# A fused attention, expert and feed-forward kernel: narrowed pieces from two places, the third pass's first weights prepared later, squares and casts one unit later

## The chip, the cores and the metric

The kernel runs on one core of a Trainium2 chip. The metric is the device time of one execution in microseconds. Engines are named as in the profile: PE (TensorE, with PEld for its weight loads), DVE (VectorE), ACT (ScalarE), POOL (GpSimd) and SP (SyncE, whose queue issues the DMAs).

## The reference

Attention with masks, an expert layer whose experts all see every token, and a feed-forward layer with squared ReLU, on 2304 tokens of width 512:

```python
x = attention(q, k, v)                     # 4 batches, 8 heads, 576 positions, 64 wide
P = exp(x @ w_gate - max); 8 times: P /= P.sum(1); P /= P.sum(0); P *= N / 8
for e in range(8):                         # w1[e]: 512 x 1024, w2[e]: 1024 x 512
    out += P[:, e:e+1] * (np.maximum(x @ w1[e], 0) @ w2[e])
r = np.maximum(out @ w_in, 0)              # w_in: 512 x 2048, given in float64
return (r * r) @ w_out                     # w_out: 2048 x 512, given in float64
```

## The kernel before, in words

**Passes and steps.** After attention the work is 80 steps. Steps 0 to 31 are the expert layer for a first 1024 tokens and a "single" group of 256 tokens (pass 1), steps 32 to 63 the expert layer for the last 1024 tokens (pass 2), steps 64 to 71 and 72 to 79 the feed-forward layer for the same two groups (passes 3 and 4). In the code `NS1` is 32, `first` is [0, 32, 64, 72], and `i` is the step. Each step covers 256 hidden columns.

**Operands.** Every float32 operand is held as a rounded high part and the remainder, and a product is three matmuls. The high part is an ACT copy (`hi`), the remainder a DVE subtraction (`lo`). Products of 1024 tokens are formed by seven smaller products (u1 to u7 for the first layer, v1 to v7 for the second where it is "mixed" in the same way), whose operands need sums of blocks; POOL forms these (`s1`, `s2` for weights, `mix` for the hidden layer).

**Units and the order written by hand.** PE's work is a list of units, each mostly six matmuls of 512 columns. `order` is the list of one step. `after(k, f)` puts `f` into the program behind the k-th following unit, so for every engine the program order is set by these numbers. Each engine, and SP's queue, runs its instructions in that order; a waiting instruction holds back what stands behind it on its engine.

**Weights of a step.** `prep_w(i)` prepares step n = i + 1: from the raw block in `raw1` it makes `blk` (high and low) and, through `sums`, `sum` (high and low), in one of two sets `wset[n % 2]`, and stores them to DRAM. A pass for the second token group (`kept`) prepares nothing and fetches the four tiles that the pass before stored. Step 64's weights are an exception before the change: they are prepared at the end of pass 1 (in step 31, in the places that belong to step 32), stored, and the weights of step 32 are fetched into the same tiles behind unit 10 of step 31. At step 63 they are fetched like any others.

**Blocks of the tokens.** The seven token operands `x_hi`, `x_lo` of the next pass are fetched by `fetch_block` in the last step of a pass, 14 transfers of 512 KB. They were prepared before by `split_on`: a load, then for each block an ACT cast and behind the next unit a DVE subtraction and two stores.

**Narrowing.** The feed-forward weights come as 64-bit floats. `load_raw` loads a piece (512 columns), `narrow` makes float32 of it with seven DVE instructions in three stages, and stage 3 ends with the store (L334) to `w32`. 22 pieces (`DEEP`) are done in steps 3 to 19, one stage behind each of the units 1, 3, 5 and 7, so 3 steps hold 4 pieces and a stage 1 stands behind unit 7 in every third step. In these the result `topf` lies in the first half of the tile `deep[2]` and a second array `x` in its other half. The pieces alternate between two source tiles, `deep[0]` and `deep[1]`. Stage 1 (L310, L314) writes `topf`; stage 2 is L319 and L322, stage 3 L327, L330 and L333. The ten later pieces write `x` into the source itself, at every second word.

**Squares.** In steps 64 to 71 and 79, `evac_g` takes a hidden tile from PSUM: `positive` (ACT, L669), then `square` (two ACT instructions, L674), then `low` (DVE, L659), each one unit after the other. The tiles `r` and `g` come from a ring of three.

**Copies that PE waits for.** u1's result is copied by ACT (L755), u4's (L767) and u5's (L771) free the bank that the next of these products writes; v1's copies are L945. L871, L875 and L955 on DVE, L867 and L869 add or copy a finished bank into `acc`, which frees the bank. In step 32 two transposes of the single group (`turn`, L905, copy L918) use the bank of w0 and w1.

Of the kernel before, what the change touches and what calls it, by code (L numbers as in the profile page):

```python
# [10 lines left out]
F32 = mybir.dt.float32  # L11
F32R = mybir.dt.float32r
I32 = mybir.dt.int32
# [23 lines left out]
NS1 = E * SPE  # L37
# [13 lines left out]
def tile_kernel(ctx: ExitStack, tc: tile.TileContext, a):  # L51
# [113 lines left out]
    def prep_w(i, layers=(1, 2)):  # L165

        out = []
        tt = nc.gpsimd.tensor_tensor
        c = lambda z, k: z[:, k, :]
        flat = lambda z: z.rearrange("p b c -> p (b c)")  # L170

        def hi(w, src):
            return lambda: nc.scalar.copy(w[0], src)

        def lo(w, src, then=lambda: None):
            def f():
                nc.vector.tensor_tensor(out=w[1], in0=src, in1=w[0].bitcast(F32), op=ALU.subtract)  # L177
                then()

            return f  # L180

        n = i + 1
        late = 4 if i == 2 * NS1 else 0
        if NS1 < n <= 2 * NS1 or first[3] <= n < len(steps):
            w = wset[n % 2]
            out += [(0, lambda: fetch("blk", n, w["blk"])), (0, lambda: fetch("sum", n, w["sum"]))]
        elif 1 in layers and n < len(steps):
            w = wset[n % 2]

            def s1():  # L190
                tt(out=c(sums, 0), in0=c(raw1, 2), in1=c(raw1, 3), op=ALU.add)
                tt(out=c(sums, 2), in0=c(raw1, 0), in1=c(raw1, 2), op=ALU.subtract)

            def s2():
                tt(out=c(sums, 1), in0=c(sums, 0), in1=c(raw1, 0), op=ALU.subtract)
                tt(out=c(sums, 3), in0=c(raw1, 1), in1=c(sums, 1), op=ALU.subtract)

            def keep(name):
                if n < 2:
                    kept_back.append(lambda: store(name, n, w[name]))  # L200
                else:
                    store(name, NS1 if n == NS1 else place(n), w[name])

            def blk_done():
                if n not in (0, NS1):
                    load_w(2 * NS1 if n + 1 == NS1 else n + 1, 0)
                keep("blk")

            at = (4, 5, 6, 8) if n == NS1 else (2, 5, 10, 12) if TURN + 1 < n < NS1 else (2, 5, 10, 14) if n < NS1 else (2, 5, 8, 11)
            spread = n > first[2] + 1  # L210
            if spread:
                at = (6, 7, 14, 16)
            out += [(3 if spread else 0, s1), (4 if spread else 1, s2), (late + at[0], hi(w["blk"], flat(raw1)))]
            out += [(late + at[1], lo(w["blk"], flat(raw1), blk_done))]
            out += [(late + at[2], hi(w["sum"], flat(sums)))]
            out += [(late + at[3], lo(w["sum"], flat(sums), lambda: keep("sum")))]
            if n == NS1:
                out += [(10, lambda: fetch("blk", n, w["blk"])), (10, lambda: fetch("sum", n, w["sum"]))]
        if 2 not in layers:
            return out  # L220
        if kept(i):
            w2 = wset[i % 2]["w2"]
            out += [(0, lambda: fetch("w2", i, w2))]
            if mixed(i):
                out += [(6 if i == NS1 else 0, lambda: fetch("mix", i, mixes[i % 2]))]
            if i == 2 * NS1 - 3:
                out += [(2, lambda: load_w(2 * NS1 + 1, 0)), (2, lambda: load_w(2 * NS1, 1))]
        elif i >= 0:
            w2 = wset[i % 2]["w2"]
            moe = i < SCALED  # L230
            r = raw2.rearrange("p (f e d) -> p f e d", f=FC, e=2)
            z = mix32.rearrange("p (k d) -> p k d", k=4)

            def m1():
                tt(out=c(z, 0), in0=r[:, 0, 1], in1=r[:, 1, 1], op=ALU.add)
                tt(out=c(z, 2), in0=r[:, 0, 0], in1=r[:, 0, 1], op=ALU.subtract)

            def m2():
                tt(out=c(z, 1), in0=c(z, 0), in1=r[:, 0, 0], op=ALU.subtract)
                tt(out=c(z, 3), in0=r[:, 1, 0], in1=c(z, 1), op=ALU.subtract)  # L240
                load_w(i + 1, 1)

            def m3():
                tt(out=r[:, 1, 1], in0=r[:, 0, 1], in1=r[:, 1, 1], op=ALU.add)  # L244
                tt(out=r[:, 0, 1], in0=r[:, 0, 0], in1=r[:, 0, 1], op=ALU.subtract)

            def m4():
                tt(out=r[:, 0, 0], in0=r[:, 1, 1], in1=r[:, 0, 0], op=ALU.subtract)
                tt(out=r[:, 1, 0], in0=r[:, 1, 0], in1=r[:, 0, 0], op=ALU.subtract)

            if SCALED <= i < NS1:
                at = (7, 8, 9, 9, 14, 16) if i > TURN else (7, 8, 9, 9, 13, 15)
            elif moe:
                at = (0, 0, 0, 1, 9, 11) if i == 0 else (8, 10, 11, 12, 16, 17) if i == 1 else (1, 3, 6, 7, 13, 15)
            else:
                at = (11, 13, 14, 14, 20, 22) if late else (14, 15, 16, 16, 21, 22) if n == first[2] + 2 else (12, 13, 14, 14, 19, 20)
            if i:
                out += [(at[0], hi(w2, raw2)), (at[1], lo(w2, raw2, lambda: store("w2", place(i), w2)))]
            if moe:
                out += [(at[2], m1), (at[3], m2)]  # L260
                out += [(at[4], hi(mixes[1], mix32)), (at[5], lo(mixes[1], mix32, lambda: store("mix", place(i), mixes[1])))]
            elif i + 1 < first[3]:
                m = mixes[1]

                def mix_done():
                    load_w(i + 1, 1)
                    store("mix", place(i), m)

                out += [(at[2], m3), (at[3], m4), (at[4], hi(m, raw2)), (at[5], lo(m, raw2, mix_done))]
        else:  # L270
            w2 = wset[0]["w2"]
            out += [(6, hi(w2, raw2)), (7, lo(w2, raw2, lambda: kept_back.append(lambda: store("w2", 0, w2))))]
        return out
# [22 lines left out]
    def narrow(n):  # L296

        which, s, k = raw_pieces[n]
        src = loaded.pop(n)
        low, high = src[:, :, 0], src[:, :, 1]  # L300
        if n < DEEP:
            if len(deep) == 2:
                deep.append(xb())
            topf, x = deep[2][:, :NP], deep[2][:, NP:]
        else:
            topf, x = apart[1] if apart else xb()[:, :NP], high.bitcast(F32)
        top, bits = topf.bitcast(I32), x.bitcast(I32)

        def stage_1():
            nc.vector.tensor_scalar(  # L310
                out=top, in0=high, scalar1=3, scalar2=0x3FFFFFFF,
                op0=ALU.logical_shift_left, op1=ALU.bitwise_and,
            )
            nc.vector.scalar_tensor_tensor(  # L314
                out=top, in0=high, scalar=-0x40000000, in1=top, op0=ALU.bitwise_and, op1=ALU.bitwise_or
            )

        def stage_2():
            nc.vector.tensor_scalar(  # L319
                out=bits, in0=high, scalar1=0x7FFFFFFF, scalar2=None, op0=ALU.bitwise_and  # L320
            )
            nc.vector.scalar_tensor_tensor(  # L322
                out=topf, in0=bits, scalar=float(0x38100000), in1=topf, op0=ALU.is_ge, op1=ALU.mult
            )

        def stage_3():
            nc.vector.tensor_scalar(  # L327
                out=bits, in0=top, scalar1=-0x800000, scalar2=None, op0=ALU.bitwise_and
            )
            nc.vector.scalar_tensor_tensor(  # L330
                out=x, in0=low.bitcast(U32), scalar=2.0**-52, in1=x, op0=ALU.mult, op1=ALU.mult
            )
            nc.vector.tensor_tensor(out=topf, in0=topf, in1=x, op=ALU.add)  # L333
            nc.sync.dma_start(w32[which, s, :, NP * k:NP * k + NP], topf)  # L334
            done[0] += 1

        return [stage_1, stage_2, stage_3]
# [310 lines left out]
    def evac_g(i, ghi, glo, src, k):  # L648
# [25 lines left out]
                nc.scalar.activation(out=z, in_=held["r"], func=AF.Square)  # L674

        after(k, positive)
        after(k + 1, square)
        after(k + 2, lambda: low(held["g"], False))

    def l1_pair(i):  # L680

# [298 lines left out]
    with tc.manual_schedule():  # L980
# [218 lines left out]
        for i in range(len(steps) + 1):  # L1199
# [23 lines left out]
            if mixed(i - 1):  # L1223
# [4 lines left out]
                    names = "v1 u1 v2 us v6 v5 u2 u3 v7 u4 v3 u5 v4 u6 u7"  # L1228
                elif i == NS1:
                    u |= zip(("w0", "w1"), l2s)  # L1230
                    names = "v1 u1 v2 w0 v6 w1 v5 u2 u3 v7 u4 v3 u5 v4 u6 u7"
                elif i in (first[1] - 1, first[2] - 1, len(steps) - 1):
                    names = "u1 v1 u2 v2 u3 u4 v6 u5 v5 u6 u7 v7 v3 v4"
                else:
# [39 lines left out]
            elif NS1 + 4 <= i < 2 * NS1 - 4:  # L1274
                split_on(1, 5, 9)
            elif 2 * NS1 < i < 2 * NS1 + 7:
                for k in {2 * NS1 + 1: (3, 8, 16), 2 * NS1 + 6: (2, 5, 8, 12, 16)}.get(i, (3, 16)):
                    split_on(2, k, k + 1)
            if i == first[2] - 2:
                for k, f in enumerate(operands_single()):  # L1280
# [109 lines left out]
```

## Time and profile before

| | us |
|---|---|
| median of 3 runs | 1959.26 |
| lowest, highest | 1959.09, 1964.13 |
| the profiled execution, its own time | 1961.56 |
| its span, first to last instruction | 1959.8 |
| granted clock over the span, share of full | 0.991 |

Times within a trace are counted from the start of the span. "Busy" is the time in which an engine executes; a gap in brackets is idle time of the engine before an instruction, with what ended it. PE's matmuls overlap, so that a matmul of 512 columns is shown as about 0.39 us although the next starts some 0.23 us after it. Windows were cut where the first matmul of a step starts.

### The profile page before, as it was taken

To read this page: it belongs to the slowest core of one execution; us is meant where nothing else is said; L and a number is where in the kernel's file an instruction comes from. 1 tells how busy PE (TensorE), PEld (TensorE's weight loads), DVE (VectorE), ACT (ScalarE), POOL (GpSimd) and SP (SyncE) were. 2 spreads that over 40 slices of the span, in tenths; PEclk is the share of its full clock that TensorE was granted. 3 is DMA by queue.
4 is the path that set the end of the run, shared out by engine and by line. 5 is a ranking of instruction groups with operands and counts; after the bars stand their busy time and mean duration, and the time that the engine had idled before them with its cause. 6 is when DMAs were issued, how large, how long until landed. Compare 5 with 4: busy or idle time off the path is not lost.

```text
span 1959.8 us, 28254 instructions
## 1 busy us (share of the span) xinstructions
PE 1902.1 (97%) x10343; PEld 1566.9 (80%) x10343; DVE 1614.9 (82%) x2424; ACT 816.0 (42%) x1354; POOL 672.6 (34%) x584
## 2 busy tenths in 40 slices
PE   8998999899999999999899999999999999999999
PEld 6777878778777888888688888888888887878887
DVE  6786877778686699999678998998999998785896
ACT  6753333233233344444243433333333365553444
POOL 3532322322332355555232433423233344330331
PEclk9999999999999999999999999999999999999999
DMA  8685767676676466666976667667576787879671
GB/s 296 224 312 190 254 223 249 234 264 234 228 254 220 166 219 222 218 223 225 389 290 241 258 252 266 242 262 280 196 260 247 299 319 285 293 280 395 230 251 67
DMA packets 162554, 492.75 MB, mean 251 GB/s; under 512 B 16928, under 2 KB 32176, under 8 KB 162416
## 3 DMA queue, kind: packets, MB, share of 16 engines
q1 hardware_dynamic: 162416, 490.96, 69.1%
q8 instruction: 81, 1.33, 0.3%
q14 instruction: 57, 0.47, 0.1%
HBM read 282.15 MB, written 208.74 MB: 250 GB/s over the span
## 4 chain that ended last, share of the span: by engine, by line
PE 62%; DVE 4%; DMA 1%; issue 1%; POOL 1%; ACT 1%; POOLq 0%; SPq 0%; DVEq 0%; ACTq 0%
PE mm L941 13%; PE pt L622 12%; PE s L622 8%; PE mm L845 8%; PE xt L622 8%; PE s L941 5%; PE xt L941 5%; PE mm L802 3%; DMA x_hi<-b_dram 1%; DMA blkh<-w_blkh 1%; DVE g L659 0%; POOL r L731 0%; DVE acc L875 0%; DVE g L702 0%; DVE s L781 0%
## 5 line engine op out<-in xcount | busy, mean ns | idle before, releaser
L845 PE MATMUL mm<-w2h,g 128*128 128x512 f32 x928 | 297.5, 402 | 28.8 <-DVE acc L871 23.2
L731 POOL TENSOR_TENSOR r<-mix,r 128x512 f32<-128x512 f32 x51 | 67.0, 1314 | 599.5 <-DVE mix L720 490.6
L702 DVE TENSOR_TENSOR g<-r,g 128x512 fp32r<-128x512 f32 x204 | 199.2, 977 | 60.1 <-ACT g L699 58.5
L845 PEld LDWEIGHTS mm<-w2h,g 128*128 128x128 f32 x928 | 174.7, 192 | 76.1 <-DVE acc L871 33.0
L699 ACT CAST g<-r 128x512 fp32r<-128x512 f32 x204 | 125.4, 621 | 227.0 <-PE mm L941 106.2
L955 DVE TENSOR_TENSOR acc<-mm,acc 128x512 f32<-128x512 f32 x298 | 190.5, 678 | 14.0 <-PE mm L941 14.0
L244 POOL TENSOR_TENSOR raw<-raw 128x256 f32<-128x256 f32 x36 | 37.1, 1031 | 437.1 <-DVE w2l L177 399.3
L845 PE MATMUL mm<-w2l,g 128*128 128x512 f32 x464 | 184.7, 398 | 0.0
L871 DVE SCALAR_TENSOR_TENSOR acc<-mm,ptile,acc 128x512 f32<-128x512 f32 x194 | 141.0, 743 | 27.3 <-PE mm L845 27.1
L699 ACT CAST g<-mix 128x512 fp32r<-128x512 f32 x153 | 94.7, 620 | 91.8 <-POOL mix L731 79.0
L622 PE MATMUL s<-x_hi,blkh 128*128 128x512 f32 x316 | 124.0, 392 | 7.9 <-DMA blkh<-w_blkh 7.9
L941 PE MATMUL mm<-g,w2h 128*128 128x512 f32 x408 | 126.4, 391 | 0.3 <-ACT s L945 0.2
L941 PE MATMUL mm<-g,mixh 128*128 128x512 f32 x408 | 125.6, 389 | 0.0
L622 PE MATMUL pt<-x_hi,sumh 128*128 128x512 f32 x316 | 123.8, 392 | 1.8 <-ACT s L767 1.8
L622 PE MATMUL xt<-x_hi,sumh 128*128 128x512 f32 x316 | 124.3, 393 | 0.5 <-DVE s L772 0.2
L622 PE MATMUL s<-x_hi,blkl 128*128 128x512 f32 x316 | 123.8, 392 | 0.0
L622 PE MATMUL s<-x_lo,blkh 128*128 128x512 f32 x316 | 123.7, 391 | 0.0
L622 PE MATMUL xt<-x_hi,suml 128*128 128x512 f32 x316 | 123.2, 390 | 0.0
L622 PE MATMUL xt<-x_lo,sumh 128*128 128x512 f32 x316 | 123.2, 390 | 0.0
L622 PE MATMUL pt<-x_lo,sumh 128*128 128x512 f32 x316 | 123.2, 390 | 0.0
L622 PE MATMUL pt<-x_hi,suml 128*128 128x512 f32 x316 | 123.1, 390 | 0.0
L802 PE MATMUL mm<-xs,blkh 128*128 128x256 f32 x624 | 113.1, 281 | 1.4 <-DVE pT L593 1.2
(265 smaller groups left out, 4900.0 us busy)
## 6 DMA issues: line engine op xcount, KB each, us to landing
raw<-in_w SPq DMA_DIRECT2D x61, 512.0 KB, 4.2
blkh<-w_blkh SPq DMA_DIRECT2D x41, 512.0 KB, 3.6
blkl<-w_blkl SPq DMA_DIRECT2D x41, 512.0 KB, 4.5
sumh<-w_sumh SPq DMA_DIRECT2D x41, 512.0 KB, 4.9
suml<-w_suml SPq DMA_DIRECT2D x41, 512.0 KB, 5.7
w_blkh<-blkh SPq DMA_DIRECT2D x40, 512.0 KB, 5.1
w_blkl<-blkl SPq DMA_DIRECT2D x40, 512.0 KB, 6.3
w_sumh<-sumh SPq DMA_DIRECT2D x40, 512.0 KB, 5.4
```

Source lines behind the costliest of these rows:

```text
L244: tt(out=r[:, 1, 1], in0=r[:, 0, 1], in1=r[:, 1, 1], op=ALU.add)
L622: nc.tensor.matmul(ps, w[:, c], z[:, x, j], start=start and k == 0, stop=stop and k == 5, skip_group_check=True)
L699: after(k, lambda: nc.scalar.copy(b[:, 0], src))
L702: lambda: nc.vector.tensor_tensor(out=b[:, 1], in0=src, in1=b[:, 0].bitcast(F32), op=ALU.subtract),
L731: sub = lambda o, x, y: nc.gpsimd.tensor_tensor(out=o, in0=x, in1=y, op=ALU.subtract)
L802: nc.tensor.matmul(ps, w[:, c], z[:, kc], start=k == 0, stop=k == len(terms) - 1)
L845: nc.tensor.matmul(ps, g[:, c0 * 128:c0 * 128 + 128], wt[:, fc], start=k == 0, stop=k == 3 * FC - 1)
L871: nc.vector.scalar_tensor_tensor(out=dst, in0=ps, scalar=p, in1=dst, op0=ALU.mult, op1=ALU.add)
L941: nc.tensor.matmul(ps, w[wt][:, c], z[:, g], start=start and k == 0, stop=stop and k == 2, skip_group_check=True)
L955: nc.vector.tensor_tensor(out=o, in0=ps, in1=o, op=ALU.add)
```

## The change

Four things change.

1. `narrow`: in the first 22 pieces `topf` lies in the first and the second half of `deep[2]` in turn, and `x` is written into the source, at every second word, as in the later pieces.
2. `prep_w`: step 31 no longer prepares step 64; it fetches the weights of step 32 behind its unit 0. Step 63 no longer fetches the weights of step 64; it prepares them (behind units 0, 1, 3, 6 and 8 of step 63) and stores them behind units 22 and 26, which lie in step 64. The raw block of step 65 is loaded after the `lo` of step 63 instead of in step 61, where that of step 64 is loaded now. In step 32 w1 and v5 change places, and the fetch of `mix` moves from unit 6 to 7.
3. `evac_g`: `square` and `low` stand one unit later.
4. The casts of `split_on` in steps 65 to 70 stand behind unit 4 instead of 3 (in step 70 also behind 1 instead of 2 and 4 instead of 5).

```diff
@@ prep_w
-        if NS1 < n <= 2 * NS1 or first[3] <= n < len(steps):
+        if NS1 <= n < 2 * NS1 or first[3] <= n < len(steps):
             w = wset[n % 2]
             out += [(0, lambda: fetch("blk", n, w["blk"])), (0, lambda: fetch("sum", n, w["sum"]))]
...
-                else:
-                    store(name, NS1 if n == NS1 else place(n), w[name])
+                elif n != 2 * NS1:
+                    store(name, place(n), w[name])
...
-                if n not in (0, NS1):
-                    load_w(2 * NS1 if n + 1 == NS1 else n + 1, 0)
+                if n:
+                    load_w(n + 1, 0)
                 keep("blk")
-            at = (4, 5, 6, 8) if n == NS1 else (2, 5, 10, 12) if TURN + 1 < n < NS1 else (2, 5, 10, 14) if n < NS1 else (2, 5, 8, 11)
+            at = (1, 3, 6, 8) if n == 2 * NS1 else (2, 5, 10, 12) if TURN + 1 < n < NS1 else (2, 5, 10, 14) if n < NS1 else (2, 5, 8, 11)
...
-            if n == NS1:
-                out += [(10, lambda: fetch("blk", n, w["blk"])), (10, lambda: fetch("sum", n, w["sum"]))]
+            if n == 2 * NS1:
+                out += [(k, lambda name=name: store(name, place(n), w[name])) for k, name in ((22, "blk"), (26, "sum"))]
...
-                out += [(6 if i == NS1 else 0, lambda: fetch("mix", i, mixes[i % 2]))]
+                out += [(7 if i == NS1 else 0, lambda: fetch("mix", i, mixes[i % 2]))]
             if i == 2 * NS1 - 3:
-                out += [(2, lambda: load_w(2 * NS1 + 1, 0)), (2, lambda: load_w(2 * NS1, 1))]
+                out += [(2, lambda: load_w(2 * NS1, 0)), (2, lambda: load_w(2 * NS1, 1))]
@@ narrow
-            topf, x = deep[2][:, :NP], deep[2][:, NP:]
+            topf = deep[2][:, NP * (n % 2):NP * (n % 2) + NP]
         else:
-            topf, x = apart[1] if apart else xb()[:, :NP], high.bitcast(F32)
-        top, bits = topf.bitcast(I32), x.bitcast(I32)
+            topf = apart[1] if apart else xb()[:, :NP]
+        top, bits, x = topf.bitcast(I32), high, high.bitcast(F32)
@@ evac_g
         after(k, positive)
-        after(k + 1, square)
-        after(k + 2, lambda: low(held["g"], False))
+        after(k + 2, square)
+        after(k + 3, lambda: low(held["g"], False))
@@ the loop over steps
                 elif i == NS1:
-                    names = "v1 u1 v2 w0 v6 w1 v5 u2 u3 v7 u4 v3 u5 v4 u6 u7"
+                    names = "v1 u1 v2 w0 v6 v5 w1 u2 u3 v7 u4 v3 u5 v4 u6 u7"
...
-                for k in {2 * NS1 + 1: (3, 8, 16), 2 * NS1 + 6: (2, 5, 8, 12, 16)}.get(i, (3, 16)):
+                for k in {2 * NS1 + 1: (4, 8, 16), 2 * NS1 + 6: (1, 4, 8, 12, 16)}.get(i, (4, 16)):
                     split_on(2, k, k + 1)
```

## Rows read from the trace of the kernel before

**Rows 1.** The page's first part: busy us, share of the span, instructions.
```profile
PE 1902.1 (97%) x10343; PEld 1566.9 (80%) x10343; DVE 1614.9 (82%) x2424; ACT 816.0 (42%) x1354; POOL 672.6 (34%) x584
```

**Rows 2.** Windows of the steps 3, 6, 9, 12, 15 and 18.
```profile
core 0: us, PE busy (x) PEld busy (x) DVE busy (x) ACT busy (x) POOL busy (x), PEclk, DMA share, GB/s
...
500.15:533.70 33.55, 28.95 (x128) 23.38 (x127) 21.44 (x31) 9.10 (x13) 7.71 (x9) 0.90 0.57 197
...
sum 193.49, PE 168.82 PEld 136.94 DVE 128.46 ACT 60.59 POOL 47.09; mean PE 28.14 PEld 22.82 DVE 21.41 ACT 10.10 POOL 7.85
```

**Rows 3.** Windows of the ten other steps between 4 and 17.
```profile
302.94:329.30 26.36, 26.27 (x128) 21.92 (x127) 22.73 (x32) 9.13 (x13) 8.66 (x9) 1.00 0.79 278
...
sum 266.58, PE 263.99 PEld 218.86 DVE 220.14 ACT 90.65 POOL 82.54; mean PE 26.40 PEld 21.89 DVE 22.01 ACT 9.06 POOL 8.25
```

**Rows 4.** Waits of PE from 158 to 619 us: us, times, longest.
```profile
PE mm L845 <- DVE acc L871: 23.2, 17, 3.0
```

**Rows 5.** Timeline around 507 to 526 us: start, us, instruction, idle before it.
```profile
510.86 0.88 SPq L334 DMA_DIRECT2D w<-xb  x1
...
517.76 0.43 DVE L310 TENSOR_SCALAR xb<-mix 128x512 int32<-128x512 int32 x1 [5.67 <-DMA w<-xb]
...
519.64 0.88 PE L845 MATMUL mm<-w2h,g 128*128 128x512 f32 x2 [3.00 <-DVE acc L871]
```

**Rows 6.** Waits of DVE in front of stage 1: us, times, longest.
```profile
DVE xb L310 <- issue: 19.6, 4, 5.2
DVE xb L310 <- DMA w<-xb: 16.3, 9, 5.7
```

**Rows 7.** Windows of the steps 30, 31, 32 and 33.
```profile
896.56:921.18 24.62, 24.62 (x122) 20.88 (x121) 22.95 (x32) 11.33 (x17) 13.52 (x12) 1.00 0.59 214
921.18:947.12 25.94, 25.33 (x123) 20.64 (x122) 23.37 (x34) 11.42 (x17) 15.90 (x14) 1.00 0.83 298
947.12:980.97 33.85, 25.23 (x106) 19.80 (x105) 18.11 (x27) 8.07 (x15) 5.04 (x3) 0.90 1.03 409
980.97:1000.01 19.04, 18.70 (x83) 15.13 (x82) 13.59 (x19) 10.42 (x19) 6.30 (x4) 1.00 0.81 316
```

**Rows 8.** The chain that ended last, 930 to 985 us: start, us, what.
```profile
946.46 9.98 DMA blkh<-w_blkh
...
964.23 0.45 PE mm L905 x4
```

**Rows 9.** Windows of the steps 65 to 70 (two of six, and the sum).
```profile
1594.77:1621.63 26.86, 26.28 (x127) 21.92 (x126) 22.99 (x29) 19.23 (x33) 12.17 (x10) 1.00 0.98 377
1621.63:1649.79 28.16, 26.99 (x129) 21.78 (x127) 23.89 (x31) 14.73 (x24) 14.06 (x15) 1.00 0.82 300
...
sum 162.43, PE 159.39 PEld 131.18 DVE 135.56 ACT 94.21 POOL 64.25; mean PE 26.56 PEld 21.86 DVE 22.59 ACT 15.70 POOL 10.71
```

**Rows 10.** Window of step 71.
```profile
1757.20:1783.21 26.01, 26.01 (x128) 21.99 (x127) 13.78 (x20) 12.07 (x20) 0.00 (x0) 1.00 1.00 381
```

**Rows 11.** Waits of PE from 1595 us to the end.
```profile
PE pt L622 <- ACT s L767: 1.2, 2, 0.9
```

**Rows 12.** One line of narrowing: minimum, median, maximum in ns.
```profile
L327 DVE TENSOR_SCALAR xb<-xb x25: 414/417/421, 167.7 to 1526.6; 128x512 int32<-128x512 int32 x25
L327 DVE TENSOR_SCALAR xb<-pp x7: 410/417/420, 1585.8 to 1741.7; 128x512 int32<-128x512 int32 x7
```

**Rows 13.** Timeline of ACT, 1548 to 1610 us.
```profile
1581.74 1.03 ACT L173 CAST blkh<-raw 128x1024 fp32r<-128x1024 f32 x1
...
1608.10 0.62 ACT L357 CAST mixh<-mix 128x512 fp32r<-128x512 f32 x1 [1.04 <-DMA mix<-y_dram]
```

**Rows 14.** The `lo` of the weights: minimum, median, maximum in ns.
```profile
L177 DVE TENSOR_TENSOR blkl<-raw,blkh x40: 1210/1217/1764, 34.0 to 1743.5; 128x1024 fp32r<-128x1024 f32 x40
```

**Rows 15.** Windows of the steps 63 and 64.
```profile
1552.92:1572.72 19.80, 19.55 (x85) 15.45 (x84) 17.59 (x28) 7.41 (x13) 8.41 (x6) 1.00 0.97 390
1572.72:1594.77 22.05, 22.05 (x109) 18.73 (x110) 21.91 (x33) 12.65 (x21) 7.88 (x7) 1.00 0.69 247
```

## The prediction

> **What bounds the kernel now.** The page comes first: PE is busy 97% of the span, DVE 82% [rows 1]. So a gain must come from the few stretches in which PE waits or runs slowly, and an engine's share over the whole says nothing of them. I then cut windows by step and looked for steps longer than their neighbours. There are three places.
>
> The first is pass 1, steps 3 to 18. Every third one, six in all, is long, with a mean of 32.2 us [rows 2]. The other ten have a mean of 26.7, a plain one 26.36 [rows 3]. The list of PE's waits names DVE's additions L871 for nearly all of it [rows 4], so DVE is late there, though it is busy only 21.4 of those 32 us. The timeline tells why: the store of a narrowed piece is issued at 510.86, and DVE then stands idle for 5.67 us in front of stage 1 of the next piece, until that store has landed, because stage 1 writes the same `topf`. Two us later PE waits 3 us for an addition queued behind it [rows 5]. Together L310 waited 36 us in 13 waits [rows 6]. Nine are put down to the store; the four for which the profile names no releaser ("issue") are as long as the longest of those and stand at the same place of the order, so I read them as the same wait. [...]
>
> The second place is the turn from pass 1 to pass 2. Step 31 takes 25.94 us where step 30 takes 24.62, and step 32 takes 33.85 [rows 7]. In the chain that ended last a fetch of the first weights takes 9.98 us and lands just as u1 can start [rows 8]. It was issued late, at 946.46, behind the stores of step 64's weights from the same tiles.
>
> The third is pass 3: steps 65 to 70 together 162.43 us [rows 9], six times step 71 would be 156.06 [rows 10]. A part of these 6.4 us is PE waiting for ACT's copy L767 [rows 11], the rest DVE being late.
>
> **Narrowed pieces.** With two places, stage 1 of a piece waits for the store of the piece before the last, behind which at least the three stages of a whole piece have been queued, six units or 8 us. The wait goes. What could be late next is the load of the source, but that is issued one whole piece earlier too. After that it is DVE's own load: 22.0 us in a plain step of 26.36 [rows 3], and the six hold no more narrowing work than the plain ones (four stages each), so I expect them to become plain steps. The term is 193.49 - 6 x 26.36 = 35.3 us. The ten others hold short waits of the same kind; they have 266.58 - 263.60 = 3.0 us over the plain length, of which I take half. Sum -36.8, bounds -33 (each of the six keeps 0.4) and -38.3.
>
> Writing `x` at every second word could make DVE slower. The later pieces do it already: L327 from a packed input to a spaced output takes 417 ns, packed to packed 417 [rows 12]. I cost it at nothing. [...]
>
> **The turn at step 32.** Steps 31 and 32 lose the late fetch. The plain length of step 31 is 24.62. That of step 32 is 16 units of 19.04 / 14 = 1.36 us (step 33 has 14) and two transposes of 0.45, 22.66 [rows 7, 8]. The excess is 1.32 + 11.19 = 12.5 us. It includes two small waits: of u5 for ACT's copy behind `hi` of the sums, and of w1 on the transposes' bank; the first goes with step 64's preparation, the second with w1 one unit later. What is late next is the DMA queue: it moves 409 GB/s, a share of 1.03, throughout step 32 and carries the token blocks too [rows 7]. Four stores of 512 KB fall away, 2.1 MB or 5.1 us at that rate; the stretch gets some 12 us shorter, so at most 7 us of transfers are pushed against their users in step 33, and step 33 itself has a share of 0.81. PE needs the token blocks in the order in which they come, several us after their turn in the queue; only the second-layer weights and the mixed ones of step 33 come close. I charge 1.5 us. Term -11, bounds -12.5 and -5.5.
>
> **The preparation at step 63.** Three prices. First, `hi` of `blk` (1.03 us [rows 13]) now stands on ACT in front of v1's copies L945, for which v2 waits already; +1.0. Second, two `lo` of 1.2 to 1.8 us [rows 14] enter a step in which DVE has 19.80 - 17.59 = 2.2 us free, and step 64 has 0.1 [rows 15]; behind them on DVE stand the additions that free v1's banks. POOL's four sums come in behind `mix`. I take +2 for both (0 to 4). [...] Third, the four stores, 2.1 MB or 5 us of queue, are put behind units 8 and 12 of step 64, ahead of the loads of `split_on` in step 65, where the share is 0.98 [rows 9]. ACT waits 1.04 us for that load now [rows 13]; behind it stand the copies that free the second layer's banks. The queue is not full just before, so I take +1.5 (0 to 5). The four fetches that go were hidden. Term +4.5, bounds 0 and +10.
>
> **Pass 3, squares and casts.** With the squares at unit 4, nothing but L767 remains on ACT when u4 ends. The waits of L767 [rows 11] should go in steps 66 to 69 and in step 79, with the slow matmuls behind them some 2.5 us. The values made one unit later are used a step later, so this costs nothing; in step 79 `low` moves behind v7's additions, with a unit to spare. DVE's lateness around narrowing stays. The cast of `split_on`, one unit later, keeps its distance to its next use. Term -2.5, bounds -6 and +1.
>
> **Sum.** -36.8 - 11 + 4.5 - 2.5 = -45.8. The profiled execution took 1961.56 us of its own, 2.3 more than the median, so 1915.8 for it and **1913.5** for a median, predicted 1913. With all bounds on the good side it is 1961.56 - 38.3 - 12.5 - 6 - 2.3 = 1902; with all on the bad side, 1961.56 - 33 - 5.5 + 10 + 1 - 2.3 = 1932.
>
> **Rivals.**
> - *The wait on the store stays*, since both halves are one tile, and stage 1 waits for any store from it. For: such a rule would need nothing but the tile's name. Against: token blocks are fetched into slices of `x_hi` while PE reads other slices without waiting. Then only 2, 3 and 4 count: 1961.56 - 9 - 2.3 = 1950, still faster by 0.5%. Chance 0.04.
> [...]
> - *Pass 3 opens worse*: the stores hold the loads back by their whole 5 us and ACT holds all four copies of the second layer's banks; the other terms as above. 1919, inside the range. Chance 0.15.
> - *Slower*: the ring of three tiles `r` and `g` is held a unit longer, so that a `positive` waits on ACT for a `low` on DVE, and every copy behind it (L767, L771, L755) is late. The price is at most a unit of 1.36 us for each of 44 evacuations in steps 64 to 71 and 79, 60 us, which would give 1973. It decides once 46 us are lost, 1.05 us for each. Against: by the order, the tile taken was read at least two units earlier, or by ACT itself, in every case. Chance 0.02.
>
> **Chances.** The forecast 0.75, pass 3 worse 0.15, the first two rivals 0.06, slower 0.02, anything else (half of it faster) 0.02. A difference under 0.3%, some 6 us, cannot be told from none here. Faster 0.96, same 0.02, slower 0.02. Range 1902 to 1932, the bounds, which leaves out the rivals at 1950 and above.
>
> **What would show it.** Steps 3 to 18 all near 26.4 us, no idle time before L310, clock 1.00 throughout; u1 of step 32 without a wait, step 32 under 24 us; step 63 one to three us longer, v2 waiting for L945; in step 65 a longer wait of L357 for its load; no wait of u5 for L767 in step 66. I am wrong if the six steps keep their length, or if DVE, relieved of its wait, is late for PE by its own work.

## The result

The changed kernel takes 1912.01 us in the median of five runs (1910.54 to 1915.18); five runs of the kernel before, beside them, have 1962.78 (1959.09 to 1964.13). The ratio is 0.9749, with a 95% interval of 0.9733 to 0.9764: 2.5% faster, well beyond the 0.26% by which the five runs of the kernel before differ. The forecast was 1913, the range 1902 to 1932. The profiled execution took 1911.93 us of its own, with a span of 1910.2, so 49.6 us less than the one of before on either count.

### The profile page after: what moved, and what is told of

It is laid out like the page before. It is cut to its first block, busy times and chain, and to the rows that moved or that the text cites. A ratio compares the mean times of both kernels' runs of the same rounds, so it can differ in the third digit from the quotient of the medians.

```text
span 1910.2 us, 28255 instructions
## 1 busy us (share of the span) xinstructions
PE 1883.8 (99%) x10343; PEld 1562.8 (82%) x10343; DVE 1611.9 (84%) x2424; ACT 816.2 (43%) x1354; POOL 671.2 (35%) x584
## 4 chain that ended last, share of the span: by engine, by line
PE 87%; DVE 7%; DMA 3%; issue 1%; ACT 1%; POOL 1%; SPq 0%; POOLq 0%; DVEq 0%; ACTq 0%
PE mm L845 18%; PE pt L622 15%; PE mm L941 14%; PE s L622 11%; PE xt L622 10%; PE mm L802 6%; PE s L941 5%; PE xt L941 5%; DMA raw<-in_w 1%; DVE acc L871 1%; PE s L445 1%; PE xt L488 1%; DVE w2l L177 1%; DVE g L655 1%; DMA w2l<-w_w2l 1%
## 5 line engine op out<-in xcount | busy, mean ns | idle before, releaser
L845 PE MATMUL mm<-w2h,g 128*128 128x512 f32 x928 | 289.9, 394 | 4.0 <-ACT acc L867 3.2
L871 DVE SCALAR_TENSOR_TENSOR acc<-mm,ptile,acc 128x512 f32<-128x512 f32 x194 | 141.1, 743 | 24.9 <-PE mm L845 24.6
L622 PE MATMUL pt<-x_hi,sumh 128*128 128x512 f32 x316 | 123.2, 390 | 1.7 <-ACT s L767 1.7
L622 PE MATMUL xt<-x_hi,sumh 128*128 128x512 f32 x316 | 123.5, 391 | 0.8 <-DVE s L772 0.8
L622 PE MATMUL s<-x_hi,blkh 128*128 128x512 f32 x316 | 123.3, 390 | 0.0
L622 PE MATMUL s<-x_lo,blkh 128*128 128x512 f32 x316 | 123.1, 390 | 0.0
L622 PE MATMUL s<-x_hi,blkl 128*128 128x512 f32 x316 | 123.0, 389 | 0.0
L622 PE MATMUL pt<-x_hi,suml 128*128 128x512 f32 x316 | 123.0, 389 | 0.0
L622 PE MATMUL xt<-x_hi,suml 128*128 128x512 f32 x316 | 123.0, 389 | 0.0
L622 PE MATMUL pt<-x_lo,sumh 128*128 128x512 f32 x316 | 123.0, 389 | 0.0
L622 PE MATMUL xt<-x_lo,sumh 128*128 128x512 f32 x316 | 122.9, 389 | 0.0
```

What stands on the lines that cost most here:

```text
L622: nc.tensor.matmul(ps, w[:, c], z[:, x, j], start=start and k == 0, stop=stop and k == 5, skip_group_check=True)
L845: nc.tensor.matmul(ps, g[:, c0 * 128:c0 * 128 + 128], wt[:, fc], start=k == 0, stop=k == 3 * FC - 1)
L871: nc.vector.scalar_tensor_tensor(out=dst, in0=ps, scalar=p, in1=dst, op0=ALU.mult, op1=ALU.add)
```

## The profile after

First the page's engine line, to be held against [rows 1].

```profile
PE 1883.8 (99%) x10343; PEld 1562.8 (82%) x10343; DVE 1611.9 (84%) x2424; ACT 816.2 (43%) x1354; POOL 671.2 (35%) x584
```

No engine does less work than before in number of instructions. DVE is busy for 1611.9 us against 1614.9, and PE for 18 us less, mostly in the steps whose granted clock was below 1.00 before (11.4 us of it in the six long steps of pass 1, 2.5 in step 32). Matmuls of one line in front of and behind the wait of 3.00 us in [rows 5], before:

```profile
516.25 0.39 PE L845 MATMUL mm<-w2l,g 128*128 128x512 f32 x1
...
520.31 0.63 PE L845 MATMUL mm<-w2l,g 128*128 128x512 f32 x1
520.74 1.05 PE L845 MATMUL mm<-w2h,g 128*128 128x512 f32 x2
521.59 0.63 PE L845 MATMUL mm<-w2l,g 128*128 128x512 f32 x1
```

Behind it they start 0.43 us apart; from 516 to 528 us the granted clock was 0.72. The gain is idle and slow time taken away from PE.

**Pass 1.** The windows of the same six steps as in [rows 2], one row and the sum:

```profile
473.12:499.47 26.35, 26.28 (x129) 21.93 (x127) 21.27 (x31) 9.13 (x13) 7.75 (x9) 1.00 0.68 249
...
sum 157.74, PE 157.41 PEld 131.61 DVE 127.90 ACT 60.64 POOL 47.28; mean PE 26.24 PEld 21.93 DVE 21.32 ACT 10.11 POOL 7.88
```

And of the ten others, as in [rows 3]:

```profile
210.90:237.26 26.36, 26.29 (x128) 21.92 (x127) 22.73 (x32) 9.12 (x13) 8.80 (x9) 1.00 0.80 279
...
368.38:394.36 25.98, 25.98 (x128) 21.99 (x127) 21.51 (x31) 8.61 (x12) 7.19 (x9) 1.00 0.85 298
...
sum 261.52, PE 261.25 PEld 219.63 DVE 219.92 ACT 90.72 POOL 82.76; mean PE 26.12 PEld 21.96 DVE 21.99 ACT 9.07 POOL 8.28
```

The six give 193.49 - 157.74 = 35.75 us, the ten 266.58 - 261.52 = 5.06, together 40.8. All sixteen last 25.98 to 26.38, at a granted clock of 1.00. Seven last 25.98 to 26.04; in them PE is busy to the last hundredth. The nine others, 26.33 to 26.38, keep one short wait each of PE's weight loads (us, times, longest):

```profile
PEld mm L845 <- DVE acc L871: 4.4, 9, 0.5
```

The timeline of step 15 at the stage 1 in front of which DVE stood idle for 5.67 us before [rows 5]:

```profile
483.83 0.74 SPq L334 DMA_DIRECT2D w<-xb  x1
...
484.98 0.42 DVE L310 TENSOR_SCALAR xb<-mix 128x512 int32<-128x512 int32 x1
```

L310 now starts 1.15 us after the store of the piece before was issued (6.9 us before), with no bracket: it waits for nothing.

**The turn.** Windows of steps 31, 32 and 33 after (before: [rows 7]), and then step 33 before, to its end:

```profile
880.41:905.03 24.62, 24.62 (x122) 20.87 (x121) 21.92 (x33) 9.54 (x15) 13.23 (x11) 1.00 0.82 299
905.03:927.77 22.74, 22.74 (x106) 18.81 (x105) 16.56 (x25) 8.01 (x15) 3.20 (x2) 1.00 1.03 416
927.77:947.62 19.85, 19.44 (x85) 15.61 (x84) 13.78 (x20) 10.93 (x20) 6.31 (x4) 1.00 1.03 401
```

```profile
980.97:1000.69 19.72, 19.38 (x86) 15.69 (x85) 14.27 (x20) 10.91 (x20) 6.30 (x4) 1.00 0.83 319
```

The window of step 33 in [rows 7] ends at 1000.01, three matmuls before the first one of step 34 at 1000.69; the whole step took 19.72 us. So 25.94 + 33.85 + 19.72 = 79.51 has become 67.21, 12.3 us less. PE is never idle in step 32, though the DMA share stays at 1.03; step 33 has gone from a share of 0.83 to 1.03 and is 0.13 us longer. PE waits there once for second-layer weights, 0.4 us, where it waited 0.3 us for DVE before.

**The opening of pass 3.** Windows of steps 63, 64 and 65 after, and then the list of PE's waits in them (us, times, longest):

```profile
1499.84:1522.81 22.97, 19.80 (x85) 15.42 (x83) 20.77 (x30) 9.28 (x15) 12.20 (x10) 1.00 0.92 353
1522.81:1545.74 22.93, 22.37 (x109) 18.61 (x109) 22.58 (x33) 12.49 (x21) 7.29 (x8) 1.00 0.62 219
1545.74:1576.82 31.08, 27.89 (x127) 23.06 (x126) 22.66 (x29) 18.94 (x33) 10.84 (x11) 0.95 1.01 401
```

```profile
PE mm L845 <- ACT acc L867: 3.2, 1, 3.2
PE mm L941 <- ACT s L945: 1.7, 2, 1.2
PE pt L622 <- ACT s L767: 1.7, 1, 1.7
```

Steps 63 and 64 were 19.80 and 22.05 [rows 15], step 65 was 26.86 [rows 9]. This part of the change costs 3.17 + 0.88 + 4.22 = 8.3 us. The timeline shows where step 65 loses most of it:

```profile
1529.27 0.92 SPq L958 DMA_DIRECT2D y_dram<-acc  x2
1538.16 0.32 SPq L334 DMA_DIRECT2D w<-pp  x1
1538.53 0.42 SPq L140 DMA_DIRECT2D w_blkh<-blkh  x1
...
1555.26 1.56 SPq L371 DMA_DIRECT2D mix<-y_dram  x2
...
1563.39 0.62 ACT L357 CAST mixh<-mix 128x512 fp32r<-128x512 f32 x1 [5.39 <-DMA mix<-y_dram]
...
1566.15 0.57 ACT L867 COPY acc<-mm 128x512 f32<-128x512 f32 x1
...
1566.77 0.73 PE L845 MATMUL mm<-w2h,g 128*128 128x512 f32 x2 [3.19 <-ACT acc L867]
```

SP stands idle for 8 us in front of the store L334 of a later narrowed piece, and issues step 64's weights behind it, from 1538.53. The load of `split_on` is issued at 1555.26 and lands 8.1 us later. ACT stands for 5.39 us in front of the cast L357; behind it in ACT's order is the copy L867 that frees a bank, and PE waits 3.19 us for that. The clock of the step is down to 0.95: from 1568.32 to 1570.88, behind that wait, six matmuls start 0.43 us apart, against 0.23 in front of it, and from 1566.77 to 1573 the granted clock is 0.73.

**The rest of pass 3.** Windows of steps 66 to 70, the last and the sum, and then two of the waits that PE's weight loads had in these steps before:

```profile
1681.05:1708.47 27.42, 26.58 (x129) 21.84 (x128) 24.47 (x34) 16.32 (x27) 13.36 (x11) 1.00 0.72 278
sum 131.65, PE 130.81 PEld 109.75 DVE 109.24 ACT 75.22 POOL 52.60; mean PE 26.16 PEld 21.95 DVE 21.85 ACT 15.04 POOL 10.52
```

```profile
PEld pt L622 <- ACT s L767: 2.6, 4, 1.4
PEld mm L845 <- DVE acc L875: 2.3, 3, 1.2
```

Before they took 162.43 - 26.86 = 135.57 [rows 9], so 3.9 us have gone. The weight loads no longer wait for L767, and 0.4 us for L875. In all: -40.8 - 12.3 + 8.3 - 3.9 = -48.7 of the 49.6. Most of the rest lies behind step 71, where the program takes 175.75 us instead of 176.59; a wait of 0.3 us for L767, the second of [rows 11], is gone there.

## The experiments

The theory: the gain of pass 1 comes from the second place for `topf` alone, that of the turn from an earlier fetch in a queue relieved of four stores, and the loss at the opening of pass 3 from stores that hold the loads back (step 65) and from the new work on ACT and DVE (step 63). The rivals: pass 1 gains from `x` having left the place, not from the second place; in the turn one half of the edit does it all; step 65 is late through the squares and casts.

**Each part alone.** The first run has only the hunk of `narrow`, the second the same hunk but with one place; both move `x` into the source (the second diff is against the first run):

```diff
-            topf, x = deep[2][:, :NP], deep[2][:, NP:]
+            topf = deep[2][:, NP * (n % 2):NP * (n % 2) + NP]
...
-        top, bits = topf.bitcast(I32), x.bitcast(I32)
+        top, bits, x = topf.bitcast(I32), high, high.bitcast(F32)
```

```diff
-            topf = deep[2][:, NP * (n % 2):NP * (n % 2) + NP]
+            topf = deep[2][:, :NP]
```

The third has only the hunks of `prep_w` and of the order of step 32, the fourth only those of `evac_g` and of the casts (some lines of each are shown):

```diff
-        if NS1 < n <= 2 * NS1 or first[3] <= n < len(steps):
+        if NS1 <= n < 2 * NS1 or first[3] <= n < len(steps):
...
-                    names = "v1 u1 v2 w0 v6 w1 v5 u2 u3 v7 u4 v3 u5 v4 u6 u7"
+                    names = "v1 u1 v2 w0 v6 v5 w1 u2 u3 v7 u4 v3 u5 v4 u6 u7"
```

```diff
-        after(k + 1, square)
-        after(k + 2, lambda: low(held["g"], False))
+        after(k + 2, square)
+        after(k + 3, lambda: low(held["g"], False))
```

*Two places alone.* 

> The kernel before with the narrowing edit alone (two places for the result, x in the source). If DVE's wait for the last store cost the long steps their length: steps 3 to 18 take 419 us together as in the changed kernel (460 before), no idle time in front of L310, and the time is 41 us shorter, ratio 0.979. If a part of the gain of these steps came from the other edits: more than 425 us for the 16 steps. The turn keeps its 12 us.

Measured: 1921.29 us, ratio 0.9801 (0.9786 to 0.9815). Steps 3 to 18 take 419.13 us, as in the whole change (419.26). The turn is as it was (79.5 us); the window of step 32 and the wait in it:

```profile
905.76:939.78 34.02, 25.70 (x107) 20.14 (x105) 18.12 (x27) 8.08 (x15) 5.05 (x3) 0.85 1.04 410
```

```profile
PE s L622 <- DMA blkh<-w_blkh: 7.6, 1, 7.6
```

*`x` in the source, one place.* 

> The kernel before with x written into the source, but the result always in the same place. If the second place made the gain: the six long steps stay at 32 us, L310 idle for some 5 us in each, and the time is that of the kernel before, ratio 1.000. If the writing in place did it (a tile less that DVE writes): the steps become shorter. [...]

Measured: 1960.19 us, ratio 0.9997 (0.9988 to 1.0006). Window of a long step, the sum of the six, then what ended the idle time before L310, and L327:

```profile
496.93:530.05 33.12, 28.80 (x128) 23.28 (x127) 21.45 (x31) 9.11 (x13) 7.70 (x9) 0.90 0.57 199
...
sum 189.89, PE 166.57 PEld 135.61 DVE 128.53 ACT 60.55 POOL 47.20; mean PE 27.76 PEld 22.60 DVE 21.42 ACT 10.09 POOL 7.87
```

```profile
  issue: 19.0, 4
  DMA w<-xb: 16.1, 10
...
L327 DVE TENSOR_SCALAR mix<-xb x11: 418/419/422, 194.1 to 620.3; 128x512 int32<-128x512 int32 x11
```

The wait stays (35 us in 14 waits, 36 in 13 before [rows 6]). The six take 3.6 us less than in the trace of before, but this execution, with 1957.34 us, was the shortest of ten, and the median is that of the kernel before. So the second place is the whole gain of part 1, and the spaced writes cost nothing: 419 ns here, 417 packed [rows 12]; the other lines of narrowing that touch `x` differ by 3 ns or less. The rival of the wait that stays for the tile's name is settled by the first run and the changed kernel, where both places lie in one tile and L310 waits for no store.

*The weights alone.* 

> The kernel before with the edits of the weights alone (step 64's first weights prepared in step 63, w1 and v5 changed, the fetch of step 32 behind unit 0). If the terms are separate: steps 31 to 33 give 12 us, steps 63 to 65 take 4 to 8 us, together 4 to 8 us shorter, ratio 0.996 to 0.998. If the loss in steps 63 to 65 comes from the squares and casts: those three steps stay at 68.7 us, as before, and the ratio is 0.994.

Measured: 1955.69 us, ratio 0.9975 (0.9965 to 0.9984). Steps 31 to 33 take 24.62, 22.74 and 19.69, so the turn gains 12.5 us; steps 63 to 65 lose 6.7. Step 65 and the sum of the three:

```profile
1586.59:1616.11 29.52, 26.62 (x128) 21.84 (x126) 23.44 (x29) 19.24 (x33) 11.42 (x10) 1.00 1.02 406
sum 75.45, PE 68.82 PEld 55.91 DVE 66.78 ACT 41.01 POOL 30.89; mean PE 22.94 PEld 18.64 DVE 22.26 ACT 13.67 POOL 10.30
```

Step 65 is long without the squares and casts having moved: L357 waits 5.0 us for its load and PE 2.8 us for L867, so the rival on them falls for this wait. In the changed kernel the step is 1.6 us longer still. There PE is busy for 27.89 us at a clock of 0.95, here for 26.62 at 1.00; why the clock fell in one run and not in the other is open.

*Squares and casts alone.* 

> The kernel before with squares, low and casts one unit later alone. If the late copy L767 cost steps 66 to 70 their excess: those five steps take 131.7 us as in the changed kernel (135.6 before), ratio 0.998. If DVE's lateness there follows from the opening of pass 3 alone: no change of these steps, ratio 1.000.

Measured: 1955.76 us, ratio 0.9984 (0.9974 to 0.9993). Steps 66 to 70:

```profile
sum 132.00, PE 130.84 PEld 109.74 DVE 110.26 ACT 75.19 POOL 52.83; mean PE 26.17 PEld 21.95 DVE 22.05 ACT 15.04 POOL 10.57
```

That is 3.6 us below the 135.57 of before; squares and casts moved together here, and no run separates them. The three parts alone give 2.0, 0.25 and 0.16%, together 2.4%; the whole gives 2.5%. The last two are below the 0.36% by which the runs of the kernel before beside them differ, so there the windows carry the reading. The parts add up, which is what should be if each acts at a place of its own.

**The turn, and the opening of pass 3.** Four versions of the changed kernel. The first stores step 64's weights earlier, the second prepares them later, the third does both, the fourth fetches step 32's weights as late as before the change:

```diff
-... for k, name in ((22, "blk"), (26, "sum"))]
+... for k, name in ((16, "blk"), (18, "sum"))]              # first and third
-at = (1, 3, 6, 8) if n == 2 * NS1 else ...
+at = (2, 7, 6, 10) if n == 2 * NS1 else ...                 # second and third
-out += [(0, lambda: fetch("blk", n, w["blk"])), (0, lambda: fetch("sum", n, w["sum"]))]
+late_f = 10 if n == NS1 else 0                              # fourth
+out += [(late_f, lambda: fetch("blk", n, w["blk"])), (late_f, lambda: fetch("sum", n, w["sum"]))]
```

*Earlier stores.* 

> The changed kernel with the stores of step 64's weights behind units 16 and 18 instead of 22 and 26, that is units 2 and 4 of step 64, when the queue is nearly empty. If step 65 is long because these stores hold back the loads of split_on: L357 waits 1 to 2 us instead of 5.4, L867 no longer stops PE, step 65 takes 27 instead of 31.1 us, 4 us shorter in all. If step 65 is long because DVE and ACT come late from step 63: it keeps 31 us.

*Later preparation.* 

> The changed kernel with the preparation in step 63 at (2, 7, 6, 10) instead of (1, 3, 6, 8): hi of blk behind v1's copies, the two lo where DVE had idle time. If step 63 is long by the place of hi and lo: v2 no longer waits 1.2 us for L945 nor u5 1.7 us for L767, steps 63 and 64 take 42 to 44 us instead of 45.9. If the sum of DVE's work sets them: 45 to 46 us, the wait moved to v1 of step 64.

*Both.* 

> The changed kernel with both, the early stores and the later preparation. If the two losses are separate: the sum of the two gains, 6 us shorter than the changed kernel, ratio to before 0.972. If the second only moves DVE's lateness into step 65: no more than the first alone.

Measured, beside a median of 1962.88 for the kernel before: earlier stores 1907.73 us (ratio 0.9719, 0.9699 to 0.9740), later preparation 1912.28 (0.9747, 0.9728 to 0.9766), both 1906.49 (0.9715, 0.9697 to 0.9734). The last is the fastest complete version here. The intervals of ratios overlap with that of the change itself, that of the later preparation wholly; the windows tell them apart. Earlier stores, steps 64 and 65:

```profile
1524.18:1547.06 22.88, 22.28 (x108) 18.60 (x109) 22.56 (x33) 12.49 (x21) 7.26 (x8) 1.00 0.84 299
1547.06:1573.51 26.45, 26.31 (x128) 21.91 (x127) 22.34 (x29) 19.01 (x33) 10.64 (x10) 1.00 0.97 373
```

The queue's timeline in the same run:

```profile
1521.80 0.32 SPq L140 DMA_DIRECT2D w_blkh<-blkh  x1
...
1551.48 0.96 SPq L371 DMA_DIRECT2D mix<-y_dram  x2
```

Step 65 falls from 31.08 to 26.45. The same bytes go out from 1521.80 on, most of them in step 64, whose DMA share rises from 0.62 to 0.84; the load L371 is issued 4.4 us after the start of step 65 instead of 9.5, and L357 waits for nothing. So the loss of step 65 was the place of the stores in the queue. Later preparation, steps 63 and 65:

```profile
1499.20:1521.23 22.03, 20.16 (x86) 15.31 (x84) 20.77 (x30) 9.40 (x15) 12.48 (x10) 1.00 0.96 379
...
1544.14:1576.85 32.71, 28.73 (x128) 23.70 (x126) 22.34 (x29) 18.95 (x33) 10.60 (x10) 0.90 0.95 379
```

Step 63 falls by 0.94 us; steps 63 and 64 together take 44.94 against 45.90, between what the two theories expected. Step 65 takes it back: it starts sooner, PE waits 4.0 us for L867 instead of 3.2, and the granted clock of the step is 0.90 instead of 0.95. So this gain ahead of a wait on the DMA queue was worth nothing until the stores were moved: with both, steps 63 to 65 take 22.02 + 22.95 + 26.41.

*The late fetch.* 

> The changed kernel with the fetch of step 32's weights behind unit 10 of step 31 again, without the preparation of step 64 there. If the old wait was the four stores that the fetch had to follow (their 5 us of queue and their landing): u1 waits 3 us or less. If it was the place behind the token blocks in the queue: u1 waits 5 to 8 us, and the time is 6 us above the changed kernel.

Measured: 1917.68 us, ratio 0.9773 (0.9754 to 0.9792). Step 32, and the wait in it (this kernel has one line more, so that L622 is L623):

```profile
907.19:935.62 28.43, 24.66 (x106) 19.66 (x105) 16.68 (x25) 8.07 (x15) 3.15 (x2) 0.94 1.04 412
```

```profile
PE s L623 <- DMA blkh<-w_blkh: 3.2, 1, 3.2
```

Without the four stores, but with the fetch at its old place, the wait is 3.2 us, against 7.6 with the stores (the first run above). So the place of the fetch gives half of step 32's gain (28.43 to 22.74). The other half (34.02 to 28.43) goes mainly to the stores that fell away; it also holds w1's exchange with v5, as a wait of 0.7 us for the transposes' copy L918 is gone too. The expectation had one cause or the other; both hold, with equal parts.

**What step 63 pays for in the preparation.** Three versions of the one with both edits: one leaves out the two low halves (DVE), one the two high halves (ACT), one all four.

```diff
-... lo(w["blk"], flat(raw1), blk_done))]
+... lo(w["blk"], flat(raw1), blk_done) if n != 2 * NS1 else blk_done)]
-... hi(w["blk"], flat(raw1)))]
+... hi(w["blk"], flat(raw1)) if n != 2 * NS1 else lambda: None)]
```

The same is done to `sum`.

*No low halves.* 

> The version with stores behind units 16 and 18 and the preparation at units 2, 6, 7 and 10, without the two low halves (DVE subtractions) of step 64's weights, so what is stored as low halves is old. In that version step 63 takes 22.02 us and step 64 22.95, against 19.80 and 22.05 before the change: 3.1 us over. Theory A (the two subtractions on DVE delay the additions that free the banks): steps 63 and 64 fall to 20.2 and 22.2 here, while leaving out the high halves alone gives only 0.5 us. Theory B (the two copies on ACT delay v1's, u4's and u5's copies): 63 and 64 stay at 21.6 and 22.7 here. Theory C (it is POOL's four sums, or the raw block's load): no change here nor in the two other runs.

*No high halves.* 

> The same version without the two high halves (ACT copies) of step 64's weights; the subtractions stay and read old values. Theory A: 63 and 64 at 21.6 and 22.8 us. Theory B: 20.4 and 22.2. Theory C: 22.0 and 22.9.

*Neither.* 

> The same version without the high and the low halves of step 64's weights; POOL's four sums, the loads and the stores stay. Theories A and B: steps 63 and 64 come back to 19.8 and 22.1 us, with some 0.3 us for POOL. Theory C: they stay near 22.0 and 22.9.

Measured, the windows of step 63, each from its own run, in this order:

```profile
1500.99:1521.95 20.96, 19.83 (x86) 15.36 (x84) 18.69 (x28) 9.29 (x15) 12.49 (x10) 1.00 0.98 383
```

```profile
1499.58:1521.58 22.00, 20.16 (x85) 15.28 (x83) 20.75 (x30) 7.50 (x13) 12.46 (x10) 1.00 0.97 381
```

```profile
1500.55:1520.35 19.80, 19.56 (x86) 15.48 (x84) 18.55 (x28) 7.41 (x13) 12.47 (x10) 1.00 0.97 382
```

Of the 2.2 us above the old 19.80, the low halves carry 1.06 by themselves, the high halves 0.02 by themselves, and both together all 2.2; POOL's sums cost PE nothing there. Step 64, 22.95 us with both edits, takes 22.01, 22.92 and 22.06 in the three runs (see the last section). None of the three theories was quite right: A named the larger cause but expected more of it in step 63, and the price of ACT's copies, 1.16 us, shows only once DVE is no longer late. The whole times (1906.27, 1906.36 and 1904.49, one run each) differ by 1.9 us, less than the four runs of the version with both edits do (2.7).

## Why the prediction came right, and where its terms were off

- **Narrowed pieces**, forecast -36.8, measured -40.8, beyond the bound of -38.3. The mechanism was the one named: all sixteen steps alike, no idle time before L310, clock 1.00, and one place alone keeps the wait. The mis-sized term is the plain length. I took a step of 26.36 as undisturbed and half of 3.0 us for the ten others; they gave 5.1, since an undisturbed step takes 25.98. The 26.36 of [rows 3] contains a wait of PE's weight loads for DVE's L871, which nine of the sixteen steps keep in the changed kernel. None of the sixteen was shorter than 26.33 before, so they could not give the plain length; step 71 could, in which PE is busy for all of its 26.01 us [rows 10].
- **The turn**, forecast -11, measured -12.3, near the bound of -12.5. Step 32 was put at 22.66 without the wait and took 22.74. Of the 1.5 us charged for transfers pushed into step 33, 0.13 came; with the weights alone step 33 did not grow (19.69). The 19.04 us from which the unit of 1.36 was taken came from a window that ended early, but steps from 34 on do take 19.04, so the unit was right by luck.
- **The preparation at step 63**, forecast +4.5, measured +8.3, inside its bounds. One of its three prices failed in size: "The queue is not full just before, so I take +1.5". It cost 4.2. The DMA share was 0.16 from 1530.2 to 1538.1, with SP waiting in front of a narrowing store L334, so the time in which the queue was "not full" could not be used by stores that stand behind that one in SP's order; sent earlier they cost nothing. The rival "pass 3 opens worse" described this, and its 1919 was reached in no run of the changed kernel (at most 1915.18), because the other terms did better; but for this term it was nearer than the forecast. The prices of `hi` and `lo`, +3.0 together, came to 3.2 in step 63. The 0.9 us of step 64 belong to no price (last section).
- **Squares and casts**, forecast -2.5, measured -3.9 in steps 66 to 70 and -0.8 behind step 71, together -4.7, inside its bounds. The waits for L767 went in steps 66 to 69 and 79, as forecast, and three of the five steps last 25.98. What the term left out are the waits for L875 on DVE: "DVE's lateness around narrowing stays" held for step 70, which keeps a wait of 0.8 us, and not for the others. The rival of a ring held too long did not happen: in the changed kernel no `positive` waits for a `low`. Of the "slow matmuls" behind the waits for L767 the trace of before shows little: after the longest, 0.94 us in step 66, the first matmul took 0.50 us, the next four 0.40 and the sixth 0.39 again, at a granted clock of 1.00.
- **The sum**: errors of -4.0, -1.3, +3.8 and -2.2 cancel in part. The total is 3.9 us under the 1915.8 that was forecast for this execution: nearer, by luck, than two of its terms deserved. That 1913 is so close to 1912.01 is luck once more: the forecast starts from a median of 1959.26 before, the runs beside the change had 1962.78, and from median to median the gain is 50.8 us against the 45.8 forecast.
- **The chances** give 0.06 to the first two rivals, 0.02 of it to a DVE slowed by writing `x` at every second word. No run shows such a cost: L327 took 419 ns with one place and 419 in the changed kernel, 417 packed [rows 12].

## What to carry to other kernels

Here a buffer written again at once kept its engine waiting until its store had landed, 5.67 us at a DMA share of 0.57, and a second place removed that wait; look for one where an engine with free time is late. Work moved to a step with free PE time must be costed by what stands behind it on the engine and in the DMA queue: the four stores were free where the queue was empty *in program order* (step 65 at 26.45 us), and cost 4.2 us behind a waiting store, though the average share of step 64 was 0.62. And before the wait on a load was mended, the 0.94 us won ahead of it was only waited away.

## What the runs showed of the hardware

**DVE and POOL beside each other.** The same subtraction L177 in step 63, in the changed kernel (with POOL's instructions around it):

```profile
1507.40 1.18 POOL L191 TENSOR_TENSOR sums<-raw 128x256 f32<-128x256 f32 x1
1508.55 1.72 POOL L192 TENSOR_TENSOR sums<-raw 128x256 f32<-128x256 f32 x1
...
1507.91 1.75 DVE L177 TENSOR_TENSOR blkl<-raw,blkh 128x1024 fp32r<-128x1024 f32 x1
```

And in the version with both edits, where it stands behind POOL's four sums:

```profile
1512.64 1.21 DVE L177 TENSOR_TENSOR blkl<-raw,blkh 128x1024 fp32r<-128x1024 f32 x1
```

Overlapped, it took 1.75 us and POOL's L192 1.72; apart, 1.21, and L192 falls to 1.19 us. The 0.9 us that step 64 lost come without the preparation too: the run with two places alone, which prepares nothing in step 63, has a step 64 of 22.92 us. Its timeline:

```profile
1531.93 1.29 POOL L731 TENSOR_TENSOR mix<-r,mix 128x512 f32<-128x512 f32 x1
...
1531.94 1.83 DVE L702 TENSOR_TENSOR g<-r,g 128x512 fp32r<-128x512 f32 x1
```

In the trace of before the same two start as close together, but there POOL's is the longer one:

```profile
1573.18 1.84 POOL L731 TENSOR_TENSOR mix<-r,mix 128x512 f32<-128x512 f32 x1
...
1573.19 0.68 DVE L702 TENSOR_TENSOR g<-r,g 128x512 fp32r<-128x512 f32 x1
```

Behind DVE's 1.83 us are additions, behind them the copies L945, and v2 waits 0.55 us for these. All 13 traces agree: in eight DVE takes 1.81 to 1.83 us there and step 64 22.88 to 22.95, in five (before, one place, squares and casts alone, and the two runs without low halves) 0.67 to 0.68 and 22.01 to 22.06. POOL's start is listed at most 0.03 us ahead of DVE's in all of them, so the starts alone do not tell which one takes longer. Without the low halves DVE's is the short one again, so the preparation can set this off, as the narrowing edit can. A difference of this kind, under 1 us in a step, can come from an edit that does no work near it.
